# A first stage written out in one order, gates by chunks partly on GpSimd, and a first MOE block by quarters

## The chip, the cores and the metric

The kernel runs on one core of a Trainium2 chip. Time is device time in microseconds (us) of one execution; a shorter time is better. The engines are TensorE (PE, with its weight loads PEld), VectorE (DVE), ScalarE (ACT), GpSimd (POOL) and SyncE (SP), which issues every DMA here. A line such as L128 is a line of the kernel before.

## The reference

An mLSTM recurrence over 768 steps for 2 batches of 8 heads of 40, then a feed-forward block and a mixture of experts on the 1536 tokens (width 320):

```python
for t in range(S):
    m_new = np.maximum(f_gate[:, :, t] + m, i_gate[:, :, t])
    f_stab = np.exp(f_gate[:, :, t] + m - m_new)
    i_stab = np.exp(i_gate[:, :, t] - m_new)
    m = m_new
    C = f_stab * C + i_stab * v_t k_t^T
    n = f_stab * n + i_stab * k_t
    y[:, :, t] = sigmoid(o_gate) * (C q_t) / np.maximum(np.abs(n . q_t), 1.0)
# MOE 1: d_ff 2048
h = x @ w_in
g = np.where(h >= 1, h, np.where(h <= -1, 0.0, (h + 1) ** 2 / 4))
x = g @ w_out
# MOE 2: 8 experts of 1024, P from softmax logits and 8 rounds of row and column scaling
out += P[:, e:e + 1] * (np.maximum(x @ w1[e], 0.0) @ w2[e])
```

## The kernel before

The recurrence is computed by chunks of 128 steps. A **tile** is a chunk of one batch: tile t is chunk t // 2 of batch t % 2, 12 tiles of 128 tokens. The gates of all heads stand as rows in `g_all` (parts g_i, g_f, g_x, g_m). `gate_logs` makes the running maximum by a scan along time and the logs by five operations, `gate_sums` sums the logs within each chunk by a scan, `gate_by_token` turns rows into columns by token matmuls (`bk_g<-cst,g_all`) and ACT's exp writes `gt` and `nla`, `gate_ends` makes `lend`. All this is done for chunk 0 first and then, in `gates_rest`, for chunks 1 to 5 in one go; `g_d` is a copy in DRAM, from which each later tile reads its decay rows G broadcast over partitions.

`attn(t)` is one tile as a generator: POOL scales the values (`vw`) and, from chunk 1 on, masks G (affine select), ACT takes exp of G head by head; PE makes scores in two halves (`bk_at<-qk`), for chunk 0 also the decay (`maskb`, `m16n`, `gl`); DVE multiplies them to A; PE sums the values (`bk_at<-vw,A`) and the update of the state Cst; DVE forms the output `sg` with the sigmoid of o_gate (`sig`); PE transposes it, and `split_x` (L118, L120) writes it as two planes XH and XL, the input of MOE 1.

MOE 1 is exact float32 by such planes of inputs and weights. Its weights come as 64-bit words and are decoded by ACT and DVE (`decode`, L226 to L233: DVE steps `dv`, `dv`, `raw`) in 18 pieces, into `wk` (w_in) and `wf` (w_out). `gemm_k` (L128) is the first product, `moe1_act` (L580 to L586) the nonlinearity, `moe1_g2` (L596 to L600) the second product. The first MOE 1 stage covers tokens 0 to 511 and the first half of d_ff (8 blocks `ff` of 128) in parts of 256 tokens and two ff: all 8 ff for tokens 0 to 255, for which tiles 0 and 1 must be done, then all 8 for tokens 256 to 511 (tiles 2 and 3). `need_w` and a credit pull weight pieces, the credit pulls tiles (`next(rest)`) between the products.

The order of the instructions of an engine is made by a scheduler from what the code emits. Before MOE 1, tiles 0 and 1 are emitted in turn, a generator step of one and then of the other, with `warm(WD)` after each: WD = 4 matmuls on zeros `wz` (L312), whose results nobody reads. W0 = 10 more stand at the start. Weight pieces are emitted at the steps in PUMP, `gates_rest` at step GP = 8, and the sigmoids of ACT by tiles 0 to 1, 2 to 6 and 7 to 11. PSUM banks are named bk_g, bk_at, bk_ax.

Of the kernel before, what the change touches and what calls it, by code (L numbers as in the profile page):

```python
# [46 lines left out]
def mlstm_moe_moe_kernel(  # L47
# [82 lines left out]
    with ExitStack() as atx:  # L130
# [38 lines left out]
        def load_tile(t):
            a = QK[t % 2]  # L170
            b = ap.tile([128, 648], F32, name="kv_t", tag="kv_t", bufs=2)
            for r in range(2):
                nc.sync.dma_start(a[r * 64 : r * 64 + 40, 0 : 2 + r : 1 + r], qk[t, r].rearrange("p (a b c) -> p a b c", a=2, b=4))
            nc.sync.dma_start(b, kvo[t][:, 0:648])
            if t < 2:
                nc.sync.dma_start(sig[:, t, :], kvo[t][:, 648:968])
                return a, b, G0 if t == 0 else wide[:, 0, :].rearrange("p (h t) -> p h t", h=8)
            if gates_done:
                load_g(t)
            return a, b, G1 if t % 2 else G0  # L180
# [688 lines left out]
```

## Time and profile before

| what | us |
|---|---|
| median of 3 runs | 990.75 |
| lowest and highest | 990.57, 992.16 |
| the profiled execution | 991.75 |
| its span in the trace | 989.9 |

The span lies 1.85 us below the time of the same execution, and that execution 1.0 above the median. The granted clock of PE is 0.998 of full speed (2.4 GHz) in the mean over the span; the slices that are below it are in the rows further down. In those rows, a time in a timeline or a chain is the start and the length of what was run there; an "x8" is eight instructions in one row; what stands in square brackets is the idle time before and what ended it.

### The profile page before, as it was taken

The page shows a single profiled execution, that of the slowest core. Times are in us where ns is not written, and L with a number is a line of the kernel's source. Part 1 is how long each engine was busy: PE and PEld are TensorE (multiplying, and loading weights), DVE is VectorE, ACT ScalarE, POOL GpSimd, SP SyncE. Part 2 cuts the span into 40 slices and gives each one's busy share as a digit, 9 for nine tenths or more (in the row PEclk, how much of TensorE's full clock was granted, in tenths as well). Part 3 has the DMA queues.
Part 4 walks back from the last instruction along what each step waited for, and adds up shares of the span by engine and source line. Part 5 has one row for each costly group of instructions (what it writes and reads, how often), then busy time and mean ns, then how long its engine had stood idle before and what let it go on. Part 6 is the DMA issues. An engine that isn't in the chain of part 4 may idle for free.

```text
span 989.9 us, 13559 instructions
## 1 busy us (share of the span) xinstructions
PE 977.3 (99%) x5518; PEld 862.2 (87%) x5525; DVE 446.7 (45%) x817; ACT 371.1 (37%) x702; POOL 38.5 (4%) x51
## 2 busy tenths in 40 slices
PE   9999999999999999999999999999999999999998
PEld 5789988888878899999899999989999999999997
DVE  7886684964563644323422532342253234222222
ACT  4876675888763224211311321231132123111111
POOL 2133320000000000000000000000000000000000
PEclk9999999999999999999999999999999999999999
DMA  9756430240021002100300310030031002000000
GB/s 242 220 161 169 142 97 1 83 117 0 1 59 59 1 1 75 44 1 12 106 1 1 88 30 1 17 102 1 1 88 30 1 17 73 1 1 1 27 27 27
DMA packets 44270, 52.55 MB, mean 53 GB/s; under 512 B 3488, under 2 KB 37648, under 8 KB 44208
## 3 DMA queue, kind: packets, MB, share of 16 engines
q1 hardware_dynamic: 44208, 51.69, 18.0%
q8 instruction: 43, 0.70, 0.3%
q14 instruction: 19, 0.16, 0.0%
HBM read 49.67 MB, written 2.01 MB: 52 GB/s over the span
## 4 chain that ended last, share of the span: by engine, by line
PE 89%; DVE 3%; ACT 3%; DMA 2%; issue 1%; POOL 1%; SPq 0%; DVEq 0%; POOLq 0%; ACTq 0%
PE bk_g L128 43%; PE bk_g L768 8%; PE bk_g L766 8%; PE bk_g L767 8%; PE bk_ax L767 3%; PE bk_ax L766 3%; PE bk_ax L768 3%; PE bk_at L412 1%; PE bk_at L432 1%; DMA raw<-in_w_dram 1%; PE bk_g L596 1%; PE bk_g L598 1%; PE bk_g L597 1%; ACT g_all L396 1%; PE bk_g L312 1%
## 5 line engine op out<-in xcount | busy, mean ns | idle before, releaser
L128 PE MATMUL bk_g<-XH,wk 128*128 128x512 f32 (+1 forms) x1240 | 399.5, 388 | 0.1
L786 DVE SCALAR_TENSOR_TENSOR lo<-bk_g,hi 128x512 fp32r<-128x512 f32 x192 | 132.7, 691 | 373.1 <-ACT hi L785 372.2
L128 PE MATMUL bk_g<-XL,wk 128*128 128x512 f32 (+1 forms) x744 | 284.8, 384 | 0.1
L785 ACT ACTIVATE hi<-bk_g 128x512 fp32r<-128x512 f32 x192 | 115.0, 599 | 449.2 <-PE bk_g L128 448.7
L128 PEld LDWEIGHTS bk_g<-XH,wk 128*128 128x128 f32 x1240 | 230.7, 188 | 43.1 <-ACT XH L118 0.9
L768 PE MATMUL bk_g<-wf,lo 128*128 128x320 f32 x576 | 177.4, 308 | 0.2 <-DVE lo L786 0.2
L766 PE MATMUL bk_g<-wf,hi 128*128 128x320 f32 x576 | 177.4, 308 | 0.0
L767 PE MATMUL bk_g<-wf,hi 128*128 128x320 f32 x576 | 177.1, 307 | 0.0
L128 PEld LDWEIGHTS bk_g<-XL,wk 128*128 128x128 f32 x744 | 139.9, 188 | 22.2 <-DVE XL L120 0.3
L766 PEld LDWEIGHTS bk_g<-wf,hi 128*128 128x128 f32 x576 | 108.0, 187 | 6.7
L767 PEld LDWEIGHTS bk_g<-wf,hi 128*128 128x128 f32 x576 | 108.1, 188 | 6.3
L768 PEld LDWEIGHTS bk_g<-wf,lo 128*128 128x128 f32 x576 | 108.0, 187 | 0.5 <-DVE lo L786 0.5
L767 PE MATMUL bk_ax<-wf,hi 128*128 128x320 f32 x192 | 59.1, 308 | 0.0
L766 PE MATMUL bk_ax<-wf,hi 128*128 128x320 f32 x192 | 59.0, 307 | 0.0
L768 PE MATMUL bk_ax<-wf,lo 128*128 128x320 f32 x192 | 58.4, 304 | 0.0
L584 DVE TENSOR_TENSOR gs<-bk_g,gs 128x512 f32<-128x512 f32 x40 | 27.6, 690 | 32.0 <-ACT gs L582 31.9
L800 DVE SCALAR_TENSOR_TENSOR acc<-bk_g,P,acc 128x320 f32<-128x320 f32 x63 | 30.8, 545 | 15.3 <-PE bk_g L768 15.3
L768 PEld LDWEIGHTS bk_ax<-wf,lo 128*128 128x128 f32 x192 | 36.0, 188 | 0.0
L766 PEld LDWEIGHTS bk_ax<-wf,hi 128*128 128x128 f32 x192 | 36.0, 188 | 0.0
L767 PEld LDWEIGHTS bk_ax<-wf,hi 128*128 128x128 f32 x192 | 35.9, 187 | 0.0
L580 ACT ACTIVATE gs<-bk_g 128x512 f32<-128x512 f32 x48 | 28.4, 591 | 19.9 <-PE bk_g L128 19.3
L570 DVE TENSOR_TENSOR wf<-raw,wf 128x640 fp32r<-128x640 f32 x32 | 26.4, 825 | 16.7 <-ACT wf L569 16.7
(253 smaller groups left out, 1009.1 us busy)
## 6 DMA issues: line engine op xcount, KB each, us to landing
raw<-in_w_dram SPq DMA_DIRECT2D x32, 320.0 KB
raw<-in_w_dram SPq DMA_DIRECT2D x32, 256.0 KB
raw<-in_w_out_dram SPq DMA_DIRECT2D x8, 640.0 KB
raw<-in_w_in_dram SPq DMA_DIRECT2D x8, 512.0 KB
raw<-in_w_dram SPq DMA_DIRECT2D x64, 64.0 KB
kv_t<-in_kvo_dram SPq DMA_DIRECT2D x12, 324.0 KB
qk<-in_qk_dram SPq DMA_DIRECT2D x24, 160.0 KB
G<-g_d SPq DMA_DIRECT2D x5, 512.0 KB
```

What stands on the lines that cost most here:

```text
L128: return [mm(dst, a, b, start=i == 0, stop=i == len(seq) - 1) for i, (a, b) in enumerate(seq)]
L312: mm(to, wz, wz[:, 0:1].to_broadcast([128, 512]), start=True, stop=True)
L396: act(out=G[:, j, :], in_=G[:, j, :], func=ACTF.Exp, bias=nla[:, c, h : h + 1])
L570: vec.tensor_tensor(out=wf[:, fs, 320:640], in0=rs[n], in1=f(wf[:, fs, 0:320]), op=ALU.subtract)
L580: act(out=t, in_=pg, func=ACTF.Relu, scale=-1.0, bias=1.0)
L584: dve_at.append(vec.tensor_tensor(out=g, in0=pg, in1=t, op=ALU.max))
L766: mm(pp[i], hi[:, ts], wf[:, ff, 0:320], start=st, stop=False)
L767: mm(pp[i], hi[:, ts], wf[:, ff, 320:640], start=False, stop=False)
L768: mm(pp[i], lo[:, ts], wf[:, ff, 0:320], start=False, stop=sp)
L785: act(out=hi, in_=pg, func=ACTF.Relu)
L786: vec.scalar_tensor_tensor(out=lo, in0=pg, scalar=0.0, in1=f(hi), op0=ALU.max, op1=ALU.subtract)
L800: vec.scalar_tensor_tensor(out=acc[:, t, :], in0=pp[i], scalar=P[:, t, e : e + 1], in1=acc[:, t, :], op0=ALU.mult, op1=ALU.add)
```

## The change

- **One order.** A wrapper hands PE's matmuls, ACT's activations and DVE's operations to the scheduler so that, while `ordered[0]` is set, each is issued after the one before it in the code. The generators of tiles 0 and 1 are replaced by functions (`values`, `scores`, `decay`, `gated`, `keys`, `values_sum`, `update`, `gate_out`, `turn`, `add_update`, `tile_x`) that are called in a list written by hand. The wrapper is why PE, ACT and DVE show one line, L69, in the rows of the changed kernel. W0 is 14, WD 3; warm matmuls are left at two places of three each besides the start.
- **Gates by chunks.** Chunk 1's gates are loaded and done alone, within that list; those of chunks 2 to 5 (`gates_rest(2, NCH)`) are loaded at its end and emitted at the end of tile 2. For both, the five operations behind the maximum are now six on POOL (`eng = gp if a else vec`): the last one, which was one DVE instruction, is a tensor_scalar and a tensor_tensor. The scans stay on DVE. The sigmoids are tiles 0 to 1, 2 to 3, and 4 to 11 (emitted in tile 3).
- **Quarters.** Three weight pieces instead of more are decoded within the list. The first MOE 1 stage goes by ff 0 to 3 of tokens 0 to 255, ff 0 to 3 of tokens 256 to 511, and then ff 4 to 7 of both; before the second it runs what is pending and then tiles 2 and 3 to their end. LAG1, the number of pending second products, is 1 instead of 2.
- **Loads.** SP issues qk and the first weight piece before the values, and more, smaller loads (230 DMAs instead of 224).

```diff
-W0 = 10
-WD = 4
+W0 = 14
+WD = 3
...
-LAG1, LAG2 = 2, 3
+LAG1, LAG2 = 1, 3
...
+    def in_order(engine, fn):
+        def call(*args, **kw):
+            with ExitStack() as s:
+                if ordered[0] and engine in newest:
+                    s.enter_context(tc.issue_after(newest[engine]))
+                r = fn(*args, **kw)
+            newest[engine] = r.ins
+            return r
+        return call
...
+        def gates_rest(c0, c1):
+            gate_logs(c0 * L, c1 * L)
+            gate_sums(c0, c1)
+            store_sums(c0, c1)
+            gate_tokens(c0, c1)
...
+            eng = gp if a else vec
+            eng.tensor_tensor(out=g_x[0:96, sl], in0=g_f[0:96, sl], in1=g_m[0:96, sl], op=ALU.add)
...
+            if a:
+                gp.tensor_scalar(out=x, in0=x, scalar1=CLAMP, scalar2=None, op0=ALU.max)
+                gp.tensor_tensor(out=q, in0=x, in1=q, op=ALU.subtract)
+            else:
+                vec.scalar_tensor_tensor(out=q, in0=x, scalar=CLAMP, in1=q, op0=ALU.max, op1=ALU.subtract)
...
+            pa = values_sum(A, vw, "at", WA if t < 5 else 0)
+            if t == 3:
+                sigmoids(4, NTILE)
...
+            tile_x(t, px)
+            if t == 2:
+                gates_rest(2, NCH)
             if t + 2 < NTILE:
...
+        sg[0] = gate_out(0, heads(pa[0]))
+        gate_sums(1, 2)
+        next(pieces[1], None)
+        px[0] = turn(sg[0], "ax")
+        add_update(0, pu[0])
+        store_sums(1, 2)
...
+        sg[1] = gate_out(1, heads(pa[1]))
+        pu[1] = update(kw[1], vw[1], "g2")
+        next(pieces[2])
+        tile_x(0, px[0])
+        warm(WD, wbank)
...
+        next(pieces[2], None)
+        warm(WD, wbank)
+        raws[0:3] = [None] * 3
+        gate_tokens(1, 2)
...
+        ordered[0] = False
-        while len(done) < 2:
-            for g in starts:
-                next(g, None)
-                warm(WD)
-            step += 1
-            if step == GP:
-                gates_rest()
-            if step in PUMP:
-                pump_w()
...
-                for o in range(0, 512, w):
-                    while len(done) * 128 < t0 + o + w:
-                        next(rest)
-                    for ff in range(hf * 8, hf * 8 + 8, nf):
+                quarters = [(ff, o) for q in (0, 4) for o in (0, 256) for ff in range(hf * 8 + q, hf * 8 + q + 4, 2)]
+                for ff, o in quarters if w < 512 else [(ff, 0) for ff in range(hf * 8, hf * 8 + 8)]:
+                    if len(done) * 128 < t0 + o + w:
+                        while w < 512 and prevs:
+                            run_prev()
+                        while len(done) * 128 < t0 + o + w:
+                            next(rest)
```

Three places of the queues. PE, the last rows before the first product of MOE 1 in the kernel before (the token matmuls of chunks 1 to 5, `bk_g<-cst,g_all`, the last transposes `bk_ax<-cst,sg`, warm matmuls on `wz`; repeated warm rows are left out):

```order
L312 MATMUL bk_g_99<-wz 128x512
L355 MATMUL bk_g_415<-cst,g_all 128x48
L356 MATMUL bk_g_415<-cst,g_all 128x48
...
L361 MATMUL bk_g_427<-cst,g_all 128x16 x5
L312 LDWEIGHTS wz
L312 MATMUL bk_g_99<-wz 128x512
...
L482 MATMUL bk_ax<-cst,sg 128x128
...
L621 MATMUL bk_g_694<-wz 128x512
L482 MATMUL bk_g_395<-cst,sg 128x128
L375 MATMUL bk_g_436<-z,cst 104x48
...
L312 MATMUL bk_g_587<-wz 128x512
L128 MATMUL bk_g_477<-XH,wk 128x256
```

And in the changed kernel:

```order
L69 MATMUL bk_g_328<-cst,sg 128x128 x3
...
L69 MATMUL bk_g_96<-wz 128x512
L69 MATMUL bk_g_348<-cst,g_all 128x48 x2
L69 MATMUL bk_g_352<-cst,g_all 128x16
...
L69 MATMUL bk_g_532<-wz 128x512
L69 MATMUL bk_at<-qk_97 128x128
L69 MATMUL bk_g_357<-z,cst 104x8
L69 MATMUL bk_at<-qk_97 128x128
...
L69 MATMUL bk_g_400<-wz 128x512
L69 MATMUL bk_g_400<-XH,wk 128x256
```

Of the token matmuls of five chunks those of one are left there (two of 48 columns and one of 16). In the whole program the warm matmuls (`bk_g<-wz`) fall from 93 to 31.

POOL, from the values of tile 2 (`vw`) to those of tile 4, in the kernel before:

```order
L389 TENSOR_TENSOR vw<-kv_t,gt 128x328
L447 TENSOR_TENSOR Cst<-Cst,lend 104x328
L391 AFFINE_SELECT G_95<-G_95 128x1024
L420 TENSOR_TENSOR kw<-kv_t,G_95 128x2x4x40
L389 TENSOR_TENSOR vw<-kv_t,gt 128x328
L391 AFFINE_SELECT g_all<-g_all 128x1024
L420 TENSOR_TENSOR kw<-kv_t,g_all 128x2x4x40
L447 TENSOR_TENSOR Cst<-Cst,lend 104x328
L389 TENSOR_TENSOR vw<-kv_t,gt 128x328
```

And in the changed kernel, from the values of tile 3 on (`g_all` 512 columns wide: the gates of chunks 2 to 5):

```order
L436 TENSOR_TENSOR vw<-kv_t,gt 128x328
L540 AFFINE_SELECT scr<-scr 128x1024
L472 TENSOR_TENSOR kw<-kv_t,scr 128x2x4x40
L376 TENSOR_TENSOR g_all<-g_all 96x512
L377 TENSOR_TENSOR g_all<-g_all 112x512
L379 TENSOR_SCALAR g_all<-g_all 80x512
L380 TENSOR_SCALAR g_all<-g_all 80x512
L384 TENSOR_SCALAR g_all<-g_all 16x512
L565 TENSOR_TENSOR Cst<-Cst,lend 104x328
L385 TENSOR_TENSOR g_all<-g_all 16x512
L436 TENSOR_TENSOR vw<-kv_t,gt 128x328
L540 AFFINE_SELECT G_92<-G_92 128x1024
```

Six operations on the gates now lie between tile 3's `kw` and tile 4's `vw`, the state's product Cst among them. Six like them, 128 wide, lie between tile 1's and tile 2's products.

PE, around tile 3's values (`bk_at<-vw,A`), in the kernel before:

```order
L432 MATMUL bk_at<-vw,A 128x41
L312 LDWEIGHTS wz
L312 MATMUL bk_g_800<-wz 128x512
L482 MATMUL bk_ax<-cst,sg 128x128
L432 MATMUL bk_at<-vw,A 128x41 x7
L442 MATMUL bk_at<-vw,kw 104x82 x4
L128 MATMUL bk_g_800<-XH,wk 128x256
L128 MATMUL bk_g_800<-XL,wk 128x256
L128 MATMUL bk_g_800<-XH,wk 128x256
L427 MATMUL bk_ax<-Cst,qk_101 128x82 x4
```

And in the changed kernel:

```order
L69 MATMUL bk_ax<-Cst,qk_98 128x82 x4
L69 MATMUL bk_at<-vw,A 128x41
L69 MATMUL bk_g_592<-cst,g_all 128x48 x2
L69 MATMUL bk_g_602<-cst,g_all 128x16
...
L69 MATMUL bk_at<-vw,A 128x41 x2
L69 MATMUL bk_g_610<-z,cst 104x32
L69 MATMUL bk_at<-vw,A 128x41 x5
L69 MATMUL bk_at<-vw,kw 104x82 x4
L69 MATMUL bk_ax<-cst,sg 128x128 x3
L69 MATMUL bk_g_711<-XH,wk 128x256
L69 MATMUL bk_g_808<-XH,wk 128x256
```

The token matmuls of chunks 2 to 5 (in the kernel before all in the first place above) stand between the first and the later value matmuls of tile 3, and the next product of MOE 1 (`XH,wk`) comes behind tile 3's transposes (`cst,sg`).

## Rows read from the trace of the kernel before

**Rows 1.** Windows of the four stretches; columns stand in its head line.

```profile
core 0: us, PE busy (x) PEld busy (x) DVE busy (x) ACT busy (x) POOL busy (x), PEclk, DMA share, GB/s
0.00:40.50 40.50, 38.04 (x225) 24.86 (x229) 30.83 (x62) 24.38 (x43) 6.23 (x15) 1.00 0.77 218
40.50:77.00 36.50, 33.28 (x249) 30.15 (x252) 31.57 (x60) 25.95 (x60) 10.46 (x11) 0.95 0.69 206
77.00:135.00 58.00, 54.96 (x436) 51.54 (x436) 41.65 (x86) 37.40 (x93) 19.21 (x22) 1.00 0.52 141
135.00:989.90 854.90, 851.03 (x4613) 755.66 (x4611) 342.68 (x612) 283.32 (x508) 2.57 (x3) 1.00 0.11 33
```

**Rows 2.** Timeline of PE at the first product of MOE 1: start, length.

```profile
40.50 0.50 PE L128 MATMUL bk_g<-XH,wk 128*128 128x256 f32 x2
```

**Rows 3.** Groups of PE from 0 to 40.5 us.

```profile
L312 PE MATMUL bk_g<-wz 128*128 128x512 bf16 x82 | 22.3, 404 | 1.3 <-DVE wz L192 1.0 <-issue 0.2
```

**Rows 4.** Chain from 0 to 45 us: start, length, what.

```profile
12.34 0.89 PE bk_at L412 x8
...
18.19 0.87 PE bk_g L312 x4
19.06 0.22 PE bk_g L404
19.28 0.41 PE bk_g L405
19.69 0.39 PE bk_g L408 x4
...
23.78 1.73 PE bk_at L432 x16
...
28.32 2.96 ACT sig L379 x2
...
37.72 1.28 ACT L357
...
41.10 3.85 PE bk_g L128 x30
```

**Rows 5.** Timeline of DVE, the gates of chunks 1 to 5.

```profile
7.66 1.55 DVE L326 TENSOR_TENSOR_SCAN g_all<-g_all 112x640 f32<-112x640 f32 x1 [0.57 <-DMA g_all<-in_gates_dram]
...
9.56 0.82 DVE L330 TENSOR_TENSOR g_all<-g_all 96x640 f32<-96x640 f32 x1
...
12.74 0.82 DVE L336 SCALAR_TENSOR_TENSOR g_all<-g_all 16x640 f32<-16x640 f32 x1
```

**Rows 6.** Timeline of POOL from 50 to 67 us.

```profile
53.24 0.74 POOL L389 TENSOR_TENSOR vw<-kv_t,gt 128x328 f32<-128x328 f32 x1
...
65.16 1.32 POOL L389 TENSOR_TENSOR vw<-kv_t,gt 128x328 f32<-128x328 f32 x1
66.44 1.09 POOL L391 TENSOR_SCALAR_AFFINE_SELECT G<-G 128x1024 f32<-128x1024 f32 x1
```

**Rows 7.** Timeline of DVE, decode steps.

```profile
41.51 0.69 DVE L230 SCALAR_TENSOR_TENSOR dv<-raw,dv 128x512 int32<-128x512 int32 x1
...
43.87 0.28 DVE L272 TENSOR_TENSOR wf<-raw,wf 128x128 fp32r<-128x128 f32 x1
...
63.19 0.82 DVE L230 SCALAR_TENSOR_TENSOR dv<-raw,dv 128x640 int32<-128x640 int32 x1
...
64.53 1.36 DVE L233 SCALAR_TENSOR_TENSOR raw<-raw,dv 128x640 int32<-128x640 int32 x1
65.81 1.86 DVE L272 TENSOR_TENSOR wf<-raw,wf 128x128 fp32r<-128x128 f32 x1
```

**Rows 8.** Windows of 5 us.

```profile
70.00:75.00 5.00, 3.42 (x18) 2.97 (x20) 4.91 (x14) 2.54 (x7) 0.74 (x1) 0.77 0.95 237
75.00:80.00 5.00, 4.95 (x35) 4.38 (x35) 3.60 (x7) 1.66 (x3) 1.58 (x3) 0.88 0.66 209
115.00:120.00 5.00, 3.90 (x24) 3.29 (x25) 2.70 (x5) 4.95 (x14) 0.00 (x0) 1.00 0.35 107
```

**Rows 9.** Timeline of PE: start, length, what, idle before.

```profile
70.93 1.13 PE L412 MATMUL bk_at<-qk 104*128 104x128 f32 x8 [1.58 <-issue]
72.49 1.81 PE L412 MATMUL bk_at<-qk 104*128 104x128 f32 x8 [0.43 <-DVE Cst L476]
```

More of the change, by code (lines that the diff above doesn't have):

```diff
@@ L169, in load_tile @@
-        def load_tile(t):
[L170 to L180, printed above, removed]
+            nc.sync.dma_start(tile_g(t), g_d[b * 8 : b * 8 + 8, (c - 1) * L : c * L].unsqueeze(0).to_broadcast([128, 8, L]))
@@ L431, in attn, with values_sum @@
+        def values_sum(A, vw, tag, n):
+            pa = bank(tag)
+            if n:
+                warm(n, pa)
             for h in range(8):
                 mm(pa[:, h * 41 : (h + 1) * 41], A[h % 2][:, h // 2, :], vw[:, h, :], start=True, stop=True)
[L433 to L450 removed]
@@ L451, in attn @@
[L451 to L460 removed]
+            return pa
@@ new lines, in attn @@
+            hv = ap.tile([128, 8, 41], F32, name="hv", tag="hv")
+            vec.tensor_tensor(
+                out=hv, in0=heads(pi), in1=gt[:, c, b * 8 : b * 8 + 8].unsqueeze(2).to_broadcast([128, 8, 41]), op=ALU.mult,
+            )
+            vec.tensor_tensor(out=hv, in0=hv, in1=heads(pa), op=ALU.add)
+            sg = gate_out(t, hv)
+            yield
+            if not last:
+                add_update(t, pu)
+            px = turn(sg, "ax")
+            yield
+            tile_x(t, px)
@@ L504, in attn_rest @@
                 g = nxt
+        gate_logs(0, L)
+        gate_sums(0, 1)
+        vw, kw, A, pa, pu, px, sg = ({} for _ in range(7))
+        pieces = [m1_piece(*M1SEQ[n], raws[n]) for n in range(3)]
+        ps_ = {}
+        ps_[0, 0] = scores(0, 0, "at")
+        next(pieces[0])
+        gate_by_token(0, 1)
+        vw[0] = values(0)
+        decay(0, 0, "g1")
+        decay(0, 1, "g1")
+        ps_[0, 1] = scores(0, 1, "at")
+        A[0] = [gated(0, hf, ps_[0, hf]) for hf in range(2)]
+        kw[0] = keys(0)
@@ new lines, in mlstm_moe_moe_kernel @@
+        next(pieces[0], None)
+        decay(1, 0, "g1")
+        decay(1, 1, "g1")
+        vw[1] = values(1)
+        for hf in range(2):
+            ps_[1, hf] = scores(1, hf, "g2")
+        A[1] = [gated(1, hf, ps_[1, hf]) for hf in range(2)]
+        kw[1] = keys(1)
+        gate_logs(L, 2 * L)
+        pa[0] = values_sum(A[0], vw[0], "at", 0)
+        next(pieces[1])
+        sigmoids(0, 2)
+        pa[1] = values_sum(A[1], vw[1], "g2", 0)
+        pu[0] = update(kw[0], vw[0], "at")
+        sg[0] = gate_out(0, heads(pa[0]))
```

338 lines of the change are left out of this document (188 added, 150 removed).

## The prediction

> **What bounds the kernel now.** I read the stages first [rows 1]: TensorE (PE) is busy over 90% of each, so the end is set by how much time PE spends on anything that is not a matmul of the program. After 135 us PE is busy 851.0 of 854.9 us and the change alters nothing there: the same matmuls in another order for MOE 1's first half, and nothing of MOE 2. The whole change is decided in the first 135 us, and there "busy" misleads: PE's 38.0 us up to the first product of MOE 1 at 40.50 [rows 2] hold 84 filling matmuls on `wz` (82 at line 312 [rows 3], two at line 621) at 0.87/4 = 0.217 us [rows 4], 18.2 us. So I keep a ledger of **fill**: PE time that is no program matmul, whether a warm matmul or a wait.
>
> Up to 40.50 us the program's own matmuls are, from the chain's pieces [rows 4]: 32 score matmuls, 32 × 0.89/8 = 3.6; four decay groups at 0.22 + 0.41 + 0.39 = 1.02, 4.1; 32 value matmuls, 2 × 1.73 = 3.5; 24 token matmuls (lines 355 and 356) at a score's 0.11, 2.7; the rest (16 updates, 6 transposes, 7 small ones) about 2.3. That is 16.2, and the fill 24.3. From 40.5 to 77, 249 matmuls start [rows 1]; each counted at the usual distance between starts of its form (3.85/30 = 0.13 for MOE 1's 256 columns [rows 4]), program work is 25.2 of 36.5, fill 11.3. From 77 to 135 the same count over 436 starts gives 50.6 of 58, fill 7.4. Together **43.0 us of fill**.
>
> The chain shows why the head is long [rows 4]: ScalarE's sigmoids of tiles 2 to 11 (2.96) stand in front of the decode of MOE 1's weights, a table load (1.28 at 37.72) in front of the first XH.
>
> **The change, part by part.** *Head.* Warm matmuls fall from 93 to 31 in the program, most of them here. They stand in PE's queue between steps, so they delay what follows; but PE at 40.5 waits for ScalarE and VectorE, so removing them alone buys little. What shortens the head is the order: chunks 2 to 5 leave it. On DVE that takes away a scan of 640 columns (1.55 [rows 5], against an estimated 1.55 × 128/640 and some overhead, 0.5, for chunk 1), the five gate operations of 640 columns (from 9.56 to 13.56, 4.0; the first and the last are in [rows 5]), and four sums. On ACT the sigmoids of 3200 columns (2.96) shrink to one of 640, an estimated 0.7. Only three weight pieces stay.
>
> The new chain, with durations from rows: qk of tile 0 takes the queue place of the wide gates that the scan at 7.66 waited for [rows 5], so I start the first scores at 7.4. PE then has four score groups and four decay groups, 7.7, in a strict queue: 15.2. Tile 1's second A product (0.69) and chunk 1's scan (0.5) end at 16.5. Six POOL operations on 128 columns follow: estimated from vw's 0.74 for 328 columns and the affine select's 1.09 for 1024 [rows 6] at 0.37 with two inputs and 0.25 with one, 1.9, plus hand-overs and waits for DVE, 3.7: 20.2. Behind them in DVE's strict order stand the sums, a piece's addition, tile 1's output (two operations of 320 columns, 0.43 each at the rate of 0.69 for 512, and three small ones: 1.5) and the third piece's decode (three operations of 512 columns, 1.8 to 2.1 at up to 0.69) [rows 7]: 24.4. ACT and DVE pass that piece back and forth to 27.3, the table load of 1.28 gives 28.6, gt and a small product lead to the **first MOE 1 matmul at 29.8**, 10.7 earlier than now. Program work before it is 16.2 − 1.8 (16 token matmuls gone) + 0.2 (two scores of tile 2) = 14.5, so the fill is **15.3** instead of 24.3.
>
> *First quarter.* Before, all four blocks of tokens 0 to 255 (two ff of 256 columns each, 32 matmuls, 3.85: 15.4) lie beside tiles 2 and 3. Now two blocks (7.7) do, and everything else of MOE 1 waits until tiles 2 and 3 are done. From 29.8 to 48 PE has those 7.7, tile 2 and half of tile 3 (a tile is about 5.3: 1.8 scores, 1.7 values, 1.8 others), 14.7 of 18.2: **fill 3.5**.
>
> *Hole.* Then tile 3 stands behind the gates of chunks 2 to 5, which tile 2's end emits. Their scan starts at about 44.0, when tile 2's output leaves DVE: 1.55 × 512/640 = 1.25. Then six POOL operations of 512 columns: 0.74 × 512/328 = 1.16 for three, 1.09 × 512/1024 = 0.57 for three, and a Cst product (0.9) between: 6.1, and the decode operations of DVE lie in their way (below), so 53.2. Four sums on DVE between decode operations of two pieces: 58.3. The token matmuls were put in PE's queue ahead of the last values of tile 3, which therefore wait with them. On ACT gt and nla are followed by a table load (1.28), the sigmoid of 2560 columns (2.96 × 2560/3200 = 2.4) and another table load (1.28); only then come `lend` and the copy that tile 3's transposes wait for: 64.6, XH at 65.8, XL and PE's next real stretch at **67.5**. Between 48 and 67.5 PE has 2.1 of token matmuls and 3.1 of tile 3: **fill 14.3**.
>
> Cost bounds that no row of before shows: POOL's one-input operation of 512 columns lies between 0.4 (below the affine select's rate, 0.54) and 1.2 (above its whole 1.09 for 1024 columns); I take 0.57, since the affine select also reads one operand [rows 6]. At the upper end the hole grows by about 3 and the head by 1; at the lower end it shrinks by 1.
>
> The DMAs that move with these steps I cost at nothing: SP issues 230 instead of 224, the wide gates are asked for at the list's end some 15 us before their scan, and the store to `g_d` and tile 4's G behind the POOL operations have until tile 4's affine select, behind the hole. Were that G late, tile 4 would be, not MOE 1, which has six blocks to run by then.
>
> *POOL against DVE.* The rows show that they exclude each other: DVE's addition of 128 columns takes 0.28 at 43.87 and 1.86 at 65.81, when POOL's product (65.16, itself 1.32 instead of 0.74) and affine select run; the decode step at 64.53 takes 1.36 instead of the 0.82 of 63.19 [rows 6, 7]. In the hole, six gate operations meet about six decode steps, each pair sharing one turn, so I add 3.1 to POOL's 6.1 and 2 to DVE's. The Trainium skill, SBUF — State Buffer, section "Who interferes with whom", makes it a rule: the second of the two to issue blocks fully until the first is through, if DVE has two SBUF inputs. By that rule the elementwise work moved to POOL frees nothing while the decode runs, and the sum is the one made here; were the rows chance, the hole would end some 5 earlier (the first rival).
>
> *After 67.5.* As from 77 now: **fill 7.4**. Weight pieces decoded in the hole can only lower it, LAG1 = 1, by which a pair's second half starts earlier, only raise it; I let the two cancel.
>
> *The clock.* Granted clock was 0.77 in 70–75 and 0.88 in 75–80, and full at 115–120 [rows 8]. It fell to 1.2 GHz after PE had stood from 69.3 with little to do (idle 1.58 and 0.43 [rows 9]): eight score matmuls begun at 70.93 take 1.13, eight begun at 72.49 take 1.81. The hole is PE idle for 14 of 19.5 us, without warms. I price it at what runs at half clock: the token matmuls and tile 3's rest (half of their 5.2 is on the path, 2.6), and about 1.7 of MOE 1's first stretch after it; and 1.4 for MOE 1's first stretch after the head's quiet 20 to 29. Together **5.7**; bounds 1.7 (one short dip as now) and 8. The Trainium skill, TensorE: Matmul & The Clock Gate, section "HAM oscillation — how this bites in real kernels", names idle gaps as what brings the clock down again; the rows at 70–75 agree, and those at 115–120 show that not every stall does.
>
> **Sum.** 15.3 + 3.5 + 14.3 + 7.4 + 5.7 = 46.2 against 43.0: 3.2 longer. Against the profiled run's own 991.75 (989.9 and 1.85 around it) that is 994.9; the profiled run lies 1.0 above the median 990.75, so **993.9** for a median.
>
> **The rivals.** *Faster:* the gate chain is quicker than I make it. If POOL's and DVE's operations pass side by side (their chains then cost 6.1 and 3 less 5), tile 3 ends at about 62, and with a shorter hole the clock costs 2.5: 15 + 3.5 + 9.3 + 7.4 + 2.5 = 37.7, 5.3 less than now, **985.4**. For it: POOL's products also take just 0.74, as at 53.24 [rows 6], and the decode steps may fall before or behind the gate operations. Against: 64.53 and 65.81 [rows 7]. It decides from a hole that ends before 64.
> *No change:* hole as worked out, but the clock costs no more than 2 to 4, since the hole is not empty: 42.5 to 44.5, **990 to 992**. For it: full clock at 115–120 [rows 8] despite a busy time of 3.90. Against: 14 idle us are more than there.
> *Much slower:* POOL's one-input operations cost 1.2: head 1, hole 3 more, **998**. For it: no row has such an operation; against: the affine select's rate.
> That the change doesn't do what it says is excluded by the queue orders shown above: POOL's rows and the 31 warms are there.
>
> **How the numbers follow.** Forecast (3 longer) 0.40, much slower 0.13, no change 0.20, faster 0.27. A time within 0.2% (2 us) of now can't be told from no change. So faster 0.27, same 0.20, slower 0.53. Range 985 to 998.5: it leaves out somewhat under half of the faster case, 0.12, and 0.08 above. The forecast's own range is 991.5 to 997, by the bounds of clock and POOL.
>
> **What would show it.** In the changed profile: the first matmul of XH near 30 (head); a stretch from about 48 to 67 with PE busy under half, POOL's wide gate operations around 45 to 53 and the table load, sigmoid, table load around 60 to 64 (hole); POOL operations of 512 columns at 1.2 and 0.6; granted clock under 0.8 in parts of 50 to 72 (clock). I am wrong if the first matmul comes later than 33, if the hole ends before 64 or is filled, or if the clock stays up through it.

## The result, and the profile after

Slower: 1004.33 us in the median of 4 runs (1003.85 to 1005.57) against 991.13 of 4 runs beside it, a ratio of 1.0134 with the interval [1.0116, 1.0151]. The forecast had the sign, but 993.9 and a range up to 998.5. The profiled execution is the one of 1004.18, span 1002.4.

The stretches of [rows 1] after the change (busy us and instructions started, then granted clock):

```profile
core 0: us, PE busy (x) PEld busy (x) DVE busy (x) ACT busy (x) POOL busy (x), PEclk, DMA share, GB/s
0.00:40.50 40.50, 34.95 (x200) 26.96 (x201) 25.96 (x54) 22.99 (x47) 12.65 (x24) 0.87 0.77 212
40.50:77.00 36.50, 23.49 (x146) 20.76 (x145) 25.67 (x50) 18.80 (x38) 16.11 (x13) 0.73 0.51 159
77.00:135.00 58.00, 55.06 (x441) 53.25 (x442) 38.91 (x80) 35.19 (x89) 17.37 (x21) 0.93 0.54 155
135.00:320.00 185.00, 183.49 (x892) 150.50 (x891) 116.75 (x200) 138.30 (x261) 5.44 (x6) 1.00 0.18 54
```

PE's timeline in the places that answer to [rows 2, 9] (start, length, what; in brackets the idle time in front and what ended it):

```profile
32.51 0.78 PE L69 MATMUL bk_g<-XH,wk 128*128 128x256 f32 x1
...
53.10 0.35 PE L69 MATMUL bk_at<-vw,A 128*128 128x41 f32 x2
60.70 1.30 PE L69 MATMUL bk_g<-cst,g_all 112*128 112x48 f32 x5 [7.26 <-DVE g_all L69]
63.97 3.77 PE L69 MATMUL bk_g<-cst,g_all 112*128 112x48 f32 x15 [1.96 <-DVE g_all L69]
67.67 1.08 PE L69 MATMUL bk_at<-vw,A 128*128 128x41 f32 x4
...
77.35 0.79 PE L69 MATMUL bk_g<-XH,wk 128*128 128x256 f32 x2 [0.58 <-ACT XH L69]
```

The first MOE 1 product is 8.0 earlier than at [rows 2]. Then tile 3's values, begun at 53.10 with two matmuls, stand for 14 us behind the token matmuls of chunks 2 to 5, and those behind DVE's sums. What the sums waited for is POOL's timeline of the gate operations, to be held against [rows 6]:

```profile
50.06 1.28 POOL L376 TENSOR_TENSOR g_all<-g_all 96x512 f32<-96x512 f32 x1 [1.62 <-DVE g_all L69]
51.41 1.16 POOL L377 TENSOR_TENSOR g_all<-g_all 112x512 f32<-112x512 f32 x1
52.66 2.25 POOL L379 TENSOR_SCALAR g_all<-g_all 80x512 f32<-80x512 f32 x1
54.99 1.50 POOL L380 TENSOR_SCALAR g_all<-g_all 80x512 f32<-80x512 f32 x1
56.56 1.48 POOL L384 TENSOR_SCALAR g_all<-g_all 16x512 f32<-16x512 f32 x1
58.13 0.73 POOL L565 TENSOR_TENSOR Cst<-Cst,lend 104x328 f32<-104x328 f32 x1
58.94 1.25 POOL L385 TENSOR_TENSOR g_all<-g_all 16x512 f32<-16x512 f32 x1
```

And DVE's, where weight pieces (`dv`, `raw`, `wk`) stand between the sums and tile 3's second product A:

```profile
48.70 1.27 DVE L69 TENSOR_TENSOR_SCAN g_all<-g_all 112x512 f32<-112x512 f32 x1
...
60.23 0.42 DVE L69 TENSOR_TENSOR_SCAN g_all<-ones,g_all 80x128 f32<-80x128 f32 x1 [5.16 <-POOL g_all L385]
60.57 0.66 DVE L69 SCALAR_TENSOR_TENSOR raw<-raw,dv 128x512 int32<-128x512 int32 x1
61.15 0.68 DVE L69 TENSOR_TENSOR wk<-raw,wk 128x512 fp32r<-128x512 f32 x1
...
64.55 0.73 DVE L69 TENSOR_TENSOR_SCAN g_all<-ones,g_all 80x128 f32<-80x128 f32 x2
65.19 0.67 DVE L69 TENSOR_TENSOR A<-bk_at,scr 128x512 f32<-128x512 f32 x1
```

The windows of the hole, for [rows 8] (columns as above): no matmul at all from 55 to 60, and half clock from 60 to 80.

```profile
50.00:55.00 5.00, 3.08 (x21) 2.11 (x19) 4.99 (x7) 1.41 (x3) 4.70 (x4) 1.00 0.55 189
55.00:60.00 5.00, 0.00 (x0) 0.00 (x0) 0.07 (x1) 0.84 (x2) 4.76 (x4) 0.73 0.00 0
60.00:65.00 5.00, 2.34 (x10) 2.05 (x10) 4.77 (x10) 1.69 (x3) 0.20 (x1) 0.50 0.30 102
...
75.00:80.00 5.00, 2.46 (x8) 1.77 (x9) 4.97 (x8) 2.10 (x5) 2.24 (x2) 0.50 1.03 305
```

MOE 1 goes on at 77.35 (forecast 67.5), at full clock only from about 85. The prediction's ledger, kept for this trace in the same way: fill up to the first product 17.7 (forecast 15.3), from there to 50.5 4.0 (3.5), to 77.35 20.9, to 90 5.3, to 135 4.8, half speed included: 52.7 against 43.0 before and 46.2 forecast. These 9.7 are most of the 12.5 us between the two spans (1002.4 and 989.9). From 135 to 320 us TensorE idles another 1.5 us, in the kernel before 0.2; the rest is not traced.

Some executions of the kernels below (10 of 24 with 14 dummies at the start and the strict order on, 6 of 38 with 22, none of 25 with 30) run at half clock through the head, as told under the hardware, and take some 4 to 12 us longer: times are given of the others, ratios with intervals over all.

### The profile page after: what moved, and what is told of

Read it like the earlier page. It is cut to its first block, busy times and chain, and to the rows that moved or that the text cites. A ratio compares the mean times of both kernels' runs of the same rounds, so it can differ in the third digit from the quotient of the medians.

```text
span 1002.4 us, 13461 instructions
## 1 busy us (share of the span) xinstructions
PE 975.7 (97%) x5465; PEld 866.7 (86%) x5465; DVE 443.9 (44%) x814; ACT 373.0 (37%) x705; POOL 51.6 (5%) x63
## 4 chain that ended last, share of the span: by engine, by line
PE 93%; DVE 3%; POOL 2%; ACT 1%; issue 1%; DMA 0%; DVEq 0%; SPq 0%; POOLq 0%
PE bk_g L69 74%; PE bk_ax L69 11%; PE bk_at L69 8%; DVE sg L69 1%; DVE den L69 0%; DMA qk<-in_qk_dram 0%; POOL g_all L379 0%; DVE Cst L69 0%; ACT scr L69 0%; DVE dv L69 0%; DVE raw L69 0%; POOL g_all L384 0%; POOL g_all L380 0%; DVE A L69 0%; POOL g_all L377 0%
## 5 line engine op out<-in xcount | busy, mean ns | idle before, releaser
L69 PE MATMUL bk_g<-XH,wk 128*128 128x512 f32 (+1 forms) x1240 | 402.7, 390 | 0.6 <-ACT XH L69 0.6
L69 DVE SCALAR_TENSOR_TENSOR lo<-bk_g,hi 128x512 fp32r<-128x512 f32 x192 | 132.7, 691 | 373.1 <-ACT hi L69 372.0
L69 PE MATMUL bk_g<-XL,wk 128*128 128x512 f32 (+1 forms) x744 | 286.2, 385 | 1.1 <-DVE XL L69 1.1
L69 ACT ACTIVATE hi<-bk_g 128x512 fp32r<-128x512 f32 x192 | 115.1, 599 | 454.2 <-PE bk_g L69 453.6
L69 PEld LDWEIGHTS bk_g<-XH,wk 128*128 128x128 f32 x1240 | 233.0, 190 | 43.5 <-ACT XH L69 1.0
L69 PE MATMUL bk_g<-wf,hi 128*128 128x320 f32 x1152 | 256.1, 308 | 0.0
L69 PEld LDWEIGHTS bk_g<-wf,hi 128*128 128x128 f32 x1152 | 199.4, 188 | 12.9
L69 PE MATMUL bk_g<-wf,lo 128*128 128x320 f32 x576 | 177.3, 308 | 0.0
L69 PEld LDWEIGHTS bk_g<-XL,wk 128*128 128x128 f32 x744 | 141.6, 190 | 23.1 <-DVE XL L69 1.4
L69 PEld LDWEIGHTS bk_g<-wf,lo 128*128 128x128 f32 x576 | 108.0, 187 | 0.2 <-DVE lo L69 0.2
L69 PE MATMUL bk_ax<-wf,hi 128*128 128x320 f32 x384 | 87.1, 308 | 0.0
L69 PEld LDWEIGHTS bk_ax<-wf,hi 128*128 128x128 f32 x384 | 64.2, 187 | 0.0
L69 ACT ACTIVATE gs<-gs 128x512 f32<-128x512 f32 x96 | 60.4, 629 | 1.9
L69 PE MATMUL bk_ax<-wf,lo 128*128 128x320 f32 x192 | 58.4, 304 | 0.0
L69 DVE TENSOR_TENSOR wf<-raw,wf 128x640 fp32r<-128x640 f32 (+2 forms) x48 | 35.9, 757 | 19.5 <-ACT wf L69 19.4
L69 DVE TENSOR_TENSOR gs<-bk_g,gs 128x512 f32<-128x512 f32 x41 | 28.3, 690 | 33.1 <-ACT gs L69 33.0
L69 ACT ACTIVATE wf<-raw 128x640 fp32r<-128x640 f32 (+2 forms) x48 | 31.0, 656 | 29.8 <-DMA raw<-in_w_dram 14.7
L69 ACT ACTIVATE wk<-raw 128x512 fp32r<-128x512 f32 (+1 forms) x42 | 26.8, 638 | 35.9 <-DMA raw<-in_w_dram 21.8
L69 ACT ACTIVATE gs<-bk_g 128x512 f32<-128x512 f32 (+1 forms) x50 | 29.7, 594 | 26.5 <-PE bk_g L69 26.0
L69 DVE SCALAR_TENSOR_TENSOR acc<-bk_g,P,acc 128x320 f32<-128x320 f32 x63 | 30.8, 545 | 15.3 <-PE bk_g L69 15.3
L69 DVE TENSOR_TENSOR wk<-raw,wk 128x512 fp32r<-128x512 f32 x40 | 27.5, 689 | 20.5 <-ACT wk L69 20.3
L69 PEld LDWEIGHTS bk_ax<-wf,lo 128*128 128x128 f32 x192 | 36.0, 188 | 0.0
```

Source lines behind the costliest of these rows:

```text
L69: r = fn(*args, **kw)
```

## The experiments

Theories: **W**, GpSimd's slow gate operations make the hole; **C**, the clock does; and, after the first runs, **D**, VectorE's order of weight pieces holds tile 3, and **W2**, the late place of the gate chain does.

**Gates of chunks 2 to 5 on VectorE.**

```diff
-            eng = gp if a else vec
+            eng = gp if a == L else vec
...
-            if a:
+            if a == L:
```

> Only the gate operations of chunks 2 to 5 go back from POOL to DVE (chunk 1 stays on POOL). Theory W, the hole is the wait for POOL: six operations that took 10.1 us there (50.06 to 60.19) cost DVE about 3.5, the sums end by about 57 instead of 65.3, tile 3's XH comes near 69 instead of 76.8, and the time falls by 6 to 9 us, to 995 to 998. Theory C, most of the loss is the half clock, which stays as long as there is any hole of 10 us: 3 us at most. Were the loss the quarters' order alone, no change.

1005.76 and 1006.87 (all four: ratio 1.0194 [1.0137, 1.025]): no gain in the time. GpSimd is empty there, and the first wait of the hole is as long, but what came behind it is shorter. The first rows are PE's timeline of that run, the last DVE's window 55 to 60:

```profile
53.00 0.35 PE L69 MATMUL bk_at<-vw,A 128*128 128x41 f32 x2
60.53 3.21 PE L69 MATMUL bk_at<-vw,A 128*128 128x41 f32 x14 [7.18 <-DVE A L69]
...
73.56 0.79 PE L69 MATMUL bk_g<-XH,wk 128*128 128x256 f32 x2
...
82.60 0.59 PE L69 MATMUL bk_at<-wz 128*128 128x512 bf16 x1 [3.31 <-DVE A L69]
```

```profile
55.00:60.00 5.00, 0.00 (x0) 0.00 (x0) 5.00 (x10) 1.77 (x3) 0.00 (x0) 0.80 0.43 131
```

VectorE, with three pieces and the gate operations in its queue, now ends the first wait itself. The rest of tile 3's values start 7.1 us earlier than in the changed kernel (60.53 against 67.67), and MOE 1 goes on 3.8 earlier (73.56 against 77.35). Then TensorE waits 3.31 us for tile 4's A, the granted clock is 0.50 again from 82 to 92, and the gain is gone. So W holds for a part of this hole and fails as a price of the time; D comes from here.

**More dummies in front of tile 3's values** (54 instead of 4, token matmuls emitted behind them).

```diff
-            gate_tokens(c0, c1)
...
-            pa = values_sum(A, vw, "at", WA if t < 5 else 0)
+            pa = values_sum(A, vw, "at", 54 if t == 3 else WA if t < 5 else 0)
             if t == 3:
+                gate_tokens(2, NCH)
```

> 50 more matmuls on zeros in PE's queue before tile 3's values, where PE stood idle from 53.4 to 60.7 (about 10.9 us of them at full clock); the token matmuls of chunks 2 to 5 are emitted behind tile 3's values for it. The waits of DVE and POOL stay. Theory C: tile 3's rest, the token matmuls and MOE 1's next stretch run at 2.4 GHz, the excess of 6.0 us that matmuls at half speed show from 50 to 90 mostly goes, the time falls by 4 to 6. Theory W alone: within 2 us of the changed kernel.

999.67 to 1001.31 (ratio 1.0111 [1.0066, 1.0156]): about 3.5 below the changed kernel, and MOE 1's products run at full speed from 77.3 on, though they start no earlier. C holds for 3 to 4 us at most: by the same edit the 16 scores of tile 4 run before 77.9 instead of from 82.60 on, so this pair of kernels does not show the clock's share alone.

**Quarters undone; sigmoid of tiles 4 to 11 one tile later.**

```diff
-                quarters = [(ff, o) for q in (0, 4) for o in (0, 256) for ff in range(hf * 8 + q, hf * 8 + q + 4, 2)]
+                quarters = [(ff, o) for o in (0, 256) for ff in range(hf * 8, hf * 8 + 8, 2)]
```

```diff
-            if t == 3:
+            if t == 4:
                 sigmoids(4, NTILE)
```

> Only the quarters are undone: all eight ff of tokens 0 to 255 before those of tokens 256 to 511, as in the kernel before. Theory Q, the hole is there because the quarters took away 7.7 us of covering work: 6 us or more faster. Theory W: the scheduler still puts the token matmuls of chunks 2 to 5 in PE's queue ahead of the added blocks, so PE waits for POOL all the same and the blocks only move: within 3 us of the changed kernel.

> Only the sigmoid of tiles 4 to 11 moves from tile 3 to tile 4. As the prediction had it, table load, sigmoid and table load (4.9 us) stand in tile 3's way: 3 to 5 us faster. By the trace of the changed kernel tile 3's copy on ACT at 75.85 waited for DVE, 2.7 us after the second table load had ended: no change within 1.5 us.

Halves: one execution of 1002.1 (ratio over four 1.0181 [1.0127, 1.0236]); sigmoid late: 1004.50 and 1004.71 (1.0164 [1.0104, 1.0224]). The sigmoid is worth nothing. For the quarters see the pair further down.

**Dummies in the head** (the `warm(3, wbank)` three times: behind tile 1's scores, tile 0's values, tile 1's values).

```diff
-W0 = 14
+W0 = 22
...
+        warm(3, wbank)
...
-        warm(WD, wbank)
+        warm(14, wbank)
```

> Changed kernel with 31 more dummy matmuls in the ordered head: 22 instead of 14 at the start, three each behind tile 1's scores and behind tile 0's and tile 1's values, 14 instead of 3 behind the third weight piece, where TensorE stood idle for 2.65 us. Theory C (the idle places of the head let the granted clock fall, and the small matmuls behind them do not bring it back): the matmuls from 30 to 38 us run at full speed, which gives back some 2 us, the first MOE 1 product starts at 32.5 to 34, and no execution is above 1007: 1001 to 1004. Rival P (TensorE is the head's bound, dummies cost what they take): the first MOE 1 product starts 3 us later or more, at 35.5 to 37, and the time is 1005 to 1009.

1003.53 to 1005.48, ratio 1.0132 [1.0115, 1.0148]: nothing, either way. The granted clock from 30 to 32 is 1.00 instead of 0.50, though from 34 to 36 it is 0.50 as before. The first product is at 32.70, no earlier, and tile 3's XH reaches PE at 77.15 instead of 77.35. Both theories missed; a fill ahead of a wait with a fixed end costs nothing.

**Gate chain moved forward.** All with the head's dummies. The scan and GpSimd's six operations right behind the head; the same with 24 dummies in front of tile 3's values; and both dummy edits without the move:

```diff
         def gates_rest(c0, c1):
-            gate_logs(c0 * L, c1 * L)
...
         load_g(2)
+        load_gates(2 * L, S)
...
-        load_gates(2 * L, S)
+        gate_logs(2 * L, S)
         ordered[0] = False
```

> The same dummies, and the scan and the six GpSimd operations of chunks 2 to 5 put right behind the ordered head (their gates loaded ahead of the third tile's decay row) instead of behind the third tile; sums and token matmuls stay where they were. Theory W2 (the hole is the lateness of the gate chain: scan at 48.7, ten us on GpSimd, then sums): the GpSimd operations end before 46, the sums no longer wait for them, tile 3's values start by 60 instead of 67.7, and the time falls by 4 to 8 against the kernel with the dummies alone. Rival D (VectorE is full of weight pieces between 50 and 60, so the second product of tile 3 comes no earlier, as where those operations stood on VectorE): tile 3's values start after 64 and the time is within 2 of the kernel with the dummies alone.

> The early scan and GpSimd operations with 24 dummies in front of tile 3's values. If both W2 and C hold, this fills what is left of the hole at full clock: 988 to 996. If D holds (VectorE sets tile 3's second product), the dummies end before the values can start and the time is 996 to 1001.

> The dummies in the head and 50 more in front of tile 3's values, with the token matmuls of chunks 2 to 5 behind those: the order of all other work stays. Theory C (half of the loss is the clock): the two gains add up, 2 in the head and 3 to 4 in the hole: 997 to 1000. Rival (each gain was the other's: a start of MOE 1 at full clock reaches the hole earlier and waits longer): not below 1000.

998.28 to 1000.83 (1.0102 [1.006, 1.0143]); 996.62 to 1001.73 (1.008 [1.0057, 1.0104]); 999.39 to 1000.01 (1.0097 [1.0068, 1.0125]). The move gave about 5 with the first product at 32.77, though it left a hole in another place, and the 24 dummies on top of it nothing clear: GpSimd's ten us now stand in front of tile 2's keys, and one sum, which the scheduler had put forward, in front of VectorE's decode. Rows of the first of the three, PE's and DVE's:

```profile
50.50 1.68 PE L69 MATMUL bk_at<-vw,kw 128*104 128x82 f32 x8 [5.68 <-POOL kw L471]
```

```profile
48.71 0.42 DVE L69 TENSOR_TENSOR_SCAN g_all<-ones,g_all 80x128 f32<-80x128 f32 x1 [4.97 <-POOL g_all L384]
```

The dummies of the head and of the hole together give what those of the hole gave alone (999.67 to 1001.31) or 1 more.

**Gate chain in the head**, where GpSimd was idle; then also the quarters undone, or weight pieces on demand; and the whole gate work of chunks 2 to 5 on VectorE behind the head:

```diff
         load_piece()
+        load_gates(2 * L, S)
         load_o(2, 4)
...
         gate_sums(1, 2)
+        gate_logs(2 * L, S)
         next(pieces[1], None)
...
```

```diff
-NPIECE = (9, 12, 18, 18, 18)
+NPIECE = (0, 12, 18, 18, 18)
```

> The dummies of the head, and the scan and the six GpSimd operations of chunks 2 to 5 moved into the head, right behind chunk 1's (their gates loaded in front of the third weight piece), where GpSimd stood idle for 9.5 us. Theory W2 (what the hole costs is that these ten us of GpSimd stand in a place where tile 2 or tile 3 waits for them; put right behind the head they only moved the hole to tile 2's keys): no idle place of TensorE over 3 us is left between 35 and 65, the first MOE 1 product comes up to 3 us later for 1.3 us of scan and the longer queue of loads, and the time is 993 to 998. Rival (the shared port: ten us of GpSimd beside a full VectorE stretch the head by as much): the first MOE 1 product starts at 38 or later and the time is 1000 to 1005.

> The same with the quarters of d_ff undone (all of d_ff for 256 tokens, then for the next 256). With the gate chain out of the way the order of MOE 1's first block is what is left: theory Q (the quarters ask for tiles 2 and 3 after two products of 256 columns instead of four, before their work can be done): tile 3's wait falls by another 2 to 4 us and the time is 1 to 4 below the kernel with quarters, 990 to 996. Rival (the halves ask for all nine weight pieces before tile 2, so VectorE decodes ahead of the tiles): the same within 1.5, or slower.

> Quarters kept, gates in the head as in the first of these, but a weight piece is decoded in the first block only when a product needs it, not one with each product: tile 3's second product then stands in front of the pieces on VectorE. Theory D (VectorE's order holds tile 3): tile 3's values start 3 us earlier or more and the time is 2 to 5 below the kernel with pieces ahead. Rival (TensorE then waits for the pieces at the second half of d_ff instead): same or up to 5 slower.

> The dummies of the head, and all gate work of chunks 2 to 5, on VectorE and with its token matmuls, back between the head and the first MOE 1 product, chunk 1 still apart on GpSimd: the undoing of the split for chunks 2 to 5. If the late gate work was the loss, the hole closes (no idle place over 3 us from 40 to 65), while the first MOE 1 product comes 4 to 8 us later than 32.7 for some 6 us of VectorE: 995 to 1001. Rival (the head grows by all that the hole gives back): 1001 to 1006.

1004.99 to 1005.59 (1.0133 [1.0115, 1.0151]); 996.96 to 999.19 (1.0063 [1.0043, 1.0083]); 993.27 to 998.91 (1.0071 [1.0042, 1.01]); 997.62 to 1000.80 (1.0092 [1.0064, 1.012]). In the first three a sum of chunk 2 again slipped forward, into the head, and the first MOE product came at about 41 in the first two. They don't test W2, but at equal heads pieces on demand are already the best of them. The fourth undoes the split for chunks 2 to 5 and gives back 4 of the 13.

**The same with the sums held in their place**, and 30 dummies at the start:

```diff
-            gate_sums(c0, c1)
+            with tc.issue_after(newest["dve"]):
+                gate_sums(c0, c1)
```

> Dummies in the head (30 at the start, so that they reach a late landing of the first q and k), the scan and GpSimd's operations of chunks 2 to 5 in the head, and the sums of chunks 2 to 5 held behind tile 2's values of X, where the changed kernel has them. Theory W2 (the lateness of the gate chain is the loss in the hole): the first MOE 1 product starts at 34 to 36 (one us of scan, some of shared port), VectorE waits for GpSimd nowhere over 1 us, tile 3's values start 10 to 12 us behind tile 2's transposes less than before, and the time is 994 to 999. Rival D (VectorE's queue of weight pieces holds tile 3 all the same): 999 to 1003.

> The same, with a weight piece of the first block decoded only when a product needs it, so that tile 3's second product stands in front of four pieces on VectorE. If VectorE's order is what is left: 2 to 5 below j1_pinned, 989 to 996. If TensorE only waits for the pieces afterwards: the same as j1_pinned within 1.5.

> The first of these with the quarters undone. The two kernels with an idle head told 6.6 us in favour of the halves (1005.3 against 998.7): if that is the quarters' own price, the time is 4 to 7 below j1_pinned, 989 to 994; if it came from where those heads ended, within 2 of j1_pinned.

Gate chain in the head: 1002.45 in the median (1.0115 [1.01, 1.013]); with pieces on demand 995.92 (1.0038 [1.0024, 1.0053]); with halves instead 1000.87 (1.009 [1.0075, 1.0105]). Here the sums keep their place, but the head pays for the move. These are PE's rows of the first product and of the next one behind tile 3, with the gate chain in the head and then with pieces on demand as well:

```profile
36.85 0.68 PE L69 MATMUL bk_g<-XH,wk 128*128 128x256 f32 x1
...
77.42 0.79 PE L69 MATMUL bk_g<-XH,wk 128*128 128x256 f32 x2 [0.58 <-ACT XH L69]
```

```profile
36.78 0.77 PE L69 MATMUL bk_g<-XH,wk 128*128 128x256 f32 x1
...
73.94 0.79 PE L69 MATMUL bk_g<-XH,wk 128*128 128x256 f32 x2 [0.58 <-ACT XH L69]
```

The first product is 4.2 us later than with the head's dummies alone (32.70). About 1.9 are the eight more dummies at the start (the first scores begin at 10.08 instead of 8.22), 1.2 the scan in VectorE's queue, and 1.2 two decode steps beside GpSimd's operations (1.31 and 0.98 instead of 0.42 and 0.69). From the first product to the next one behind tile 3 it is 40.6 us instead of 44.8 in the changed kernel, and 37.2 on demand. GpSimd is through at 36, and VectorE's timeline shows a part of what is left of the hole: steps of two pieces stand between tile 2's XL, the sums and tile 3's A, at 62.76 and 63.44 where 60.23 to 65.19 was:

```profile
58.39 0.56 DVE L69 TENSOR_TENSOR XL<-bk_ax,XH 128x384 fp32r<-128x384 f32 x1
58.86 0.82 DVE L69 SCALAR_TENSOR_TENSOR dv<-raw,dv 128x640 int32<-128x640 int32 x1
59.60 0.68 DVE L69 TENSOR_TENSOR wk<-raw,wk 128x512 fp32r<-128x512 f32 x1
60.20 0.82 DVE L69 SCALAR_TENSOR_TENSOR raw<-raw,dv 128x640 int32<-128x640 int32 x1
60.93 1.90 DVE L69 TENSOR_TENSOR_SCAN g_all<-ones,g_all 80x128 f32<-80x128 f32 x4
62.76 0.66 DVE L69 TENSOR_TENSOR A<-bk_at,scr 128x512 f32<-128x512 f32 x1
```

D held. W2 gave 4.3 in the hole, and the longer head left 2 of it in the time. Pieces on demand then give 6.5 in the median; the profiled execution, the slowest of its five, shows 3.5 of them at 73.94. The quarters' own price is 1.6 here; the 6.6 of the pair with the spoiled heads did not come back.

**The strict order undone** (`ordered[0]` never set).

```diff
-        ordered[0] = True
```

> The changed kernel with the strict order undone and nothing else: the scheduler places the same instructions of the head by its own estimates. If the strict order brings its gain (the first MOE 1 product at 32.5 instead of 40.5), the product starts at 35 or later and the time rises by 2 to 6, 1006 to 1011. Rival (the emission in the new order does it, the strictness adds nothing): first product at 31 to 34 and 1002 to 1006.

1009.91 (1.0184 [1.0169, 1.0199]), first product at 40.71: undoing the strict order costs 8.2 at the first product and 5.6 at the end. The granted clock of this execution is 0.50 from 20 to 42 (in the changed kernel it is 0.50 for some 10 us before 38), so a part of the 8.2 is the clock.

**Pieces on demand alone, and everything together** (gate chain in the head, pieces on demand, dummies in the head, 9 in front of tile 3's values, 12 (`n` below) in front of its transposes; the first is the NPIECE edit above on the changed kernel).

```diff
-        def turn(sg, tag):
+        def turn(sg, tag, n=0):
             px = bank(tag)
+            warm(n, px)
...
```

> The changed kernel with one number changed: in MOE 1's first block a weight piece is decoded when a product needs it, not one with each product. With the gates in the head this gave 6.5 us (1002.45 to 995.92). Theory D (VectorE's order holds tile 3, wherever the gates are): tile 3's second product starts below 63.5 instead of at 65.19 and the time is 999 to 1002. Rival (with the gates late, the sums behind GpSimd hold that product whatever stands in front of it): within 1.5 of 1004.3.

> All at once: dummies in the head, gates of chunks 2 to 5 in the head, weight pieces on demand, the token matmuls of chunks 2 to 5 behind tile 3's values, nine dummies in front of these values and twelve in front of tile 3's transposes. If late tokens and the half clock are what is left of j2_pinned_demand (its values of tile 3 start at 63.6 behind 3.3 us of token matmuls, its hole from 60 to 77 is at half speed): values by 61, the clock at full until 75, and 988 to 993, the kernel before's 991 within reach. If a wait takes their place, as in most of the runs so far, 993 to 997.

On demand alone: 1002.2 and 1003.16 (1.0172 [1.0125, 1.0218] over all four), 1 to 3 us; A's second product moves only from 65.19 to 63.04, since the sums behind GpSimd (60.55) hold it. All together: 992.51 of 12 runs against 992.12 of 17, 1.0008 [0.9996, 1.0019], the same as the kernel before. PE's timeline there:

```profile
55.77 1.13 PE L69 MATMUL bk_at<-qk 104*128 104x128 f32 x8 [0.89 <-DVE Cst L69]
56.85 2.12 PE L69 MATMUL bk_at<-wz 128*128 128x512 bf16 x8
58.81 0.31 PE L69 MATMUL bk_at<-vw,A 128*128 128x41 f32 x2
59.12 1.12 PE L69 MATMUL bk_ax<-Cst,qk 104*128 104x82 f32 x8
60.08 2.27 PE L69 MATMUL bk_g<-cst,g_all 112*128 112x48 f32 x20
62.28 1.76 PE L69 MATMUL bk_at<-vw,A 128*128 128x41 f32 x14
...
70.13 0.50 PE L69 MATMUL bk_g<-XH,wk 128*128 128x256 f32 x2 [0.58 <-ACT XH L69]
```

The token matmuls still stand in front of the values (the edit did not move them), but at full speed: 2.27 for 20, where 15 took 3.77. So what sets this kernel apart from the one with gate chain and pieces on demand is nearly the dummies alone: MOE 1 goes on at 70.13 instead of 73.94. The first product is at 36.80, as in the kernels with the gate chain in the head.

## Why the prediction was wrong

**What held.** The place (9.7 of the 12.5 us lie before 135), the mechanism of the hole (tile 3's values behind token matmuls, sums, POOL and a scan), its sign, and that the clock falls in it. Head: 17.7 of fill instead of 15.3, first product 32.51 instead of 29.8; of these 2.7, 1.4 are there when GpSimd's six operations end (21.63 instead of 20.2). *Weight pieces decoded in the hole can only lower* the later fill did not show: from 77.35 to 135 it was 10.1, half speed included, against 7.4 and 1.7 for the clock. The sentence also hid the real point (below).

**The step that failed: the hole's end, 67.5, came at 77.35.** By the prediction's own chain: the scan started at 48.70, not 44.0 (+4.7, of which 2.7 the later head); the span from scan to the last POOL operation took 11.5, not 9.2 (+2.3); the sums 5.1 as forecast; and from there to MOE 1's next product 12.1, not 9.2 (+2.9). Sum 9.9.

- *POOL's one-input price*, taken as 0.57 with an upper bound of 1.2: 2.25, 1.50, 1.48, together 3.5 more; in the head 0.97, 0.54 and 0.57 instead of 0.25. The nearest row, the affine select, was of another kind. It is not the port: in the first kernel with the gate chain in the head (sums not yet held), VectorE stands still from 29.1 to 34.4, and the two such operations that begin there at 29.93 and 31.50 take 1.49 and 1.48. The two-input ones, 1.28, 1.16 and 1.25, were forecast at 1.16 each.
- *Errors that cancel.* That the 3.5 show as only 2.3 is luck. By its own terms (44.0, 1.25, 6.1, 3.1) the prediction's 53.2 should have been 54.4. And the 3.1 for taking turns with VectorE were hardly paid: the 2.25 is at most 0.27 above the same operation elsewhere (1.98), VectorE's decode steps at 53.79 and 54.39 took their usual 0.68 beside it, and from 55.1 on VectorE stood still. The sums' 5.1 are luck too. They were forecast as 3 and 2 for GpSimd beside them; no GpSimd operation ran there, and six decode steps in the queue took 4.1 of the 5.1. (The first quarter's 14.7 is also 0.5 to 0.9 low by its own terms.)
- *The tail.* The step "only then come `lend` and the copy that tile 3's transposes wait for" is wrong for the copy: the table loads and the sigmoid end at 72.95 and `lend` follows, but the copy starts at 75.85 and waits for DVE's `sg`; the sigmoid put off is worth nothing. The 12.1 are 15 token matmuls and 14 values at half speed, and DVE's output behind them.
- *What was not in the sum:* VectorE's queue as a holder of its own. I counted five us of sums "between decode operations" as part of POOL's chain. The profiled executions show what each holder is worth in the hole:

| kernel | first product | next product behind tile 3 | between |
|---|---|---|---|
| changed | 32.51 | 77.35 | 44.8 |
| gates of chunks 2 to 5 on VectorE | 32.79 | 73.56 | 40.8 |
| pieces on demand alone | 33.30 | 75.67 | 42.4 |
| gate chain in the head | 36.85 | 77.42 | 40.6 |
| both of these | 36.78 | 73.94 | 37.2 |
| everything together | 36.80 | 70.13 | 33.3 |

  The POOL chain is worth 4.1 to 4.3 there, the piece order 2.5, both 7.7: the two stand one behind the other and nearly add. In the time they gave 2, 1 to 3, and together 8.4 (1004.33 to 995.92), since the chain's gain was paid in the head, or lost in the next wait where the gates were on VectorE. Of the 8.4, 3.4 are there at the next product and 2.4 more at the end of the profiled execution; the rest is not traced. The faster rival was wrong on the same point: without the POOL chain MOE 1 went on at 73.56, not before 64.
- *The clock*, 5.7: matmuls at half speed cost 3.4 between 20 and 38.5 and 6.0 between 50.5 and 90, counted as length over the length at full speed. Up to 32.5 it was free (the head's dummies raised the clock there and gave nothing); the dip behind it stayed with these dummies (0.50 from 34 to 36), so its price is not shown. Of the second part 3 to 4 came back with dummies, against 4.3 forecast for it: for the time the price was right in size, the stretch (60 to 84) was not.

**Where the 13.2 went**, each time against the kernel before measured beside it: the changed kernel lies 13.2 above it, with the gate chain in the head 10.7, with pieces on demand as well 4.2, with the dummies in front of tile 3's values and transposes 0.4. So nothing is left of the head's gain. But in that last kernel the first product comes at 36.80 and not at 32.51. The 8.0 are 3.7 there, and of these 1.8 are token matmuls that only moved (16 at the prediction's 0.11). Where the other 2 us go stays open; TensorE still idles 3.03 in that head behind a table load.

## What to carry to other kernels

When a wait has a long chain behind it, write down every engine's part in series: here GpSimd's operations, then the pieces in VectorE's queue, then TensorE's matmuls at half clock. Price an edit by the part that it takes out, less what it adds at the place where the work goes. Moving work to an idle engine is worth its own operation's price there: take it from a row of the same operation, or leave the range wide. Ending a stage earlier, or running it at a higher clock, gains only if the end of the next wait moves with it. And when a term of the sum comes out as forecast, look whether it did so for the reason that was given.
